# Linear attention inside a three-stage kernel: the sums over keys computed with the features stationary and v, widened by a column of ones, moving

## The chip, the cores and the metric

One core of a Trainium2 chip runs the whole program. The metric is the device time in microseconds of one execution. The kernel before takes 2109.36 us, the median of three runs (2109.34 to 2110.07).

## The reference

Three stages follow each other: attention with exponential features, a squared-ReLU feed-forward layer, and a mixture of eight experts whose gates are balanced by eight row and column normalisations. The change lies in the first stage.

```python
def _attn_ref(q, k, v, w_phi):            # q, k, v: 4 x 8 x 576 x 64; w_phi: 64 x 128
    def phi(x):
        proj = np.einsum('bhsd,df->bhsf', x, w_phi)
        proj = proj - np.max(np.abs(proj), axis=-1, keepdims=True)
        return np.concatenate([np.exp(proj), np.exp(-proj)], axis=-1)
    q_p, k_p = (phi(q), phi(k))
    kv = np.einsum('bhsf,bhsd->bhfd', k_p, v)
    z = np.sum(k_p, axis=2)
    num = np.einsum('bhsf,bhfd->bhsd', q_p, kv)
    den = np.einsum('bhsf,bhf->bhs', q_p, z)[..., None] + 1e-06
    return (num / den).astype(np.float32)

def _moe_ref(x, w_in, w_out):             # x: 2304 x 512, hidden width 2048
    h = np.maximum(x @ w_in, 0.0)
    return (h * h @ w_out).astype(np.float32)
...
```

## The kernel before

**Units.** The attention stage runs over 16 units (NU), each one batch entry and two heads. For a unit, k and v (576 rows a head) lie as four full tiles of 128 rows and one of 64 rows (MT = 4, R0 = 64). q is handled turned, with the features on the partitions.

**Steps of a unit.** Ten small functions, s_kT to s_fin, each write out one step:

- turn_k turns k (tiles pskT), proj_k multiplies it by w_phi (psk), subtracts the largest absolute value and takes both exponentials: ek, rows on the partitions, two heads h, two signs a, 128 features;
- split_q and turn_q turn q (psqT), proj_q makes psq, and, through a reduction over partitions on GpSimd, eq: one tile for each of two halves of the rows (c) and each head (h), features on the partitions, both signs;
- kv_sum (L336) sums over the rows. For each tile and head, v is the stationary operand (64 columns) and ek the moving one (256 columns): kvp, with head h on the partitions 64h to 64h + 63, so that the two heads use the two halves of the array's columns. The sums z come from a second set of matmuls with 32 columns of ones stationary: zp, four groups of 32 partitions for two heads and even and odd tiles. ScalarE copies both to SBUF as kvs;
- kv_turn (L369) turns the four 128 x 128 pieces of kvs on TensorE (kzp), and VectorE copies out kv, adds the two parts of z (zs) and repeats it 32 times (z): now the features are on the partitions;
- numerators (L398) multiplies for each c: four matmuls psn (kv stationary, 64 columns, the two heads in two column tiles, the two signs added up) and four matmuls psd (z stationary, 32 columns, four column tiles); ScalarE copies out nm and dn, and the denominators go through DRAM as comp;
- recip divides, writes rden to DRAM and reads it back on all partitions as rb; finish multiplies nm by rb and writes xh and xl, the two halves of the next stage's input.

**What sets the order.** The steps of all units are sorted by planned times (a unit every TU = 17.54 us, offsets OFFS), and written in that order. A scheduler in the framework then orders every engine's instructions by a simulation of the timeline, so that the instructions of one step may stand apart. PSUM has three banks for the tiles of kv_sum, kv_turn and numerators (pool pc, PCB = 3) and three for those of the turns and projections (pa). v has two buffers (VAB = 2); kv_sum issues the load of v two units ahead, on SyncE's queue, in front of the copies. Into the attention stage the kernel weaves the first pass of the feed-forward layer (first_l1, first_l2; tiles ps, lines 244 to 246): half a batch entry of it can start when the four units of this entry are finished. HOLD keeps some of these halves behind the kv_sum of a named unit, by kv_sum's last instruction.

All operands of kvp, zp, psn and psd are f32. In the trace one such matmul is two instructions, each a weight load (LDWEIGHTS) and a MATMUL; these are called passes here.

## Time and profile before

| | |
|---|---|
| median of three runs | 2109.36 us |
| the profiled execution | 2109.05 us |
| its span | 2107.3 us |
| TensorE busy (PE) | 2065.6 us, 98% |
| weight loads (PEld) | 1929.1 us, 92% |
| VectorE (DVE) | 1734.0 us, 82% |
| ScalarE (ACT) | 873.1 us, 41% |
| GpSimd (POOL) | 767.5 us, 36% |
| TensorE's clock, mean granted share | 0.994 |

The attention stage fills the first 290 us, its end reaches to about 310 us; the rest of the first feed-forward pass goes on to about 350 us, the other passes to 665 us, and the experts fill what is left. Matmuls are pipelined and their ends are modelled, so the distance from one start to the next says more than a busy share. In the rows, PE is the matmul side of TensorE, PEld its weight loads. A matmul's shape such as 128*64 128x256 gives rows and columns of the stationary operand, then partitions and columns of the moving one. "Idle before" in square brackets is the time for which the engine stood still, with what ended it.

### The profile page before, as it was taken

Reading aid. Unit: us, or ns where it says so; the run is one execution under the profiler, and the core shown is the slowest. Engines: PE = TensorE matmul, PEld = TensorE weight load, DVE = VectorE, ACT = ScalarE, POOL = GpSimd, SP = SyncE. Lnnn points to the kernel's source line nnn. Section 1 sums busy time; section 2 is a strip of 40 time slices with the busy share of each in tenths; the row PEclk is TensorE's granted clock in tenths of the full one; section 3 lists DMA queues with packets and bytes.
Section 4 is the critical chain, followed back from the end, with each engine's and each line's share of the span. In section 5 each row is a group of like instructions: output and inputs, shape, how many; then the busy total and the mean of one; then the engine's idle time right before and its main releaser. Section 6 shows DMA issues by size and latency. Waiting matters only on the chain.

```text
span 2107.3 us, 31771 instructions
## 1 busy us (share of the span) xinstructions
PE 2065.6 (98%) x12411; PEld 1929.1 (92%) x12411; DVE 1734.0 (82%) x2154; ACT 873.1 (41%) x1503; POOL 767.5 (36%) x425
## 2 busy tenths in 40 slices
PE   8999999999999999999999999999999999999998
PEld 5556679888999999999999999999999999999998
DVE  4888655766566886998989989899898998989986
ACT  6786744222233654433433333333343333433332
POOL 3343300010104443443544444444444444444431
PEclk9999999999999999999999999999999999999999
DMA  4444231100135456667676776666766666676663
GB/s 112 114 101 120 74 124 60 60 31 31 55 156 206 174 200 216 202 226 253 222 229 206 226 255 220 225 222 222 247 227 220 227 223 238 224 228 234 212 201 122
DMA packets 184052, 376.40 MB, mean 179 GB/s; under 512 B 73440, under 2 KB 114272, under 8 KB 183904
## 3 DMA queue, kind: packets, MB, share of 16 engines
q1 hardware_dynamic: 183904, 374.38, 54.1%
q8 instruction: 99, 1.62, 0.3%
q14 instruction: 49, 0.40, 0.1%
HBM read 349.26 MB, written 24.93 MB: 178 GB/s over the span
## 4 chain that ended last, share of the span: by engine, by line
PE 85%; DVE 8%; DMA 3%; ACT 1%; issue 1%; SPq 1%; POOL 1%; DVEq 0%; ACTq 0%; POOLq 0%
PE psa L858 30%; PE psb L858 30%; PE ps L244 6%; PE ps L245 6%; PE ps L246 6%; PE kvp L353 2%; PE psn L409 1%; PE zp L360 1%; DMA rb<-rden 1%; DVE xl L594 1%; DVE hv L594 1%; PE psd L418 1%; DVE w2v L594 1%; DVE acc L974 1%; DMA xl<-xv 1%
## 5 line engine op out<-in xcount | busy, mean ns | idle before, releaser
L858 PE MATMUL psb<-xl,xh 128*128 128x384 f32 x2400 | 447.7, 336 | 7.4 <-DMA xl<-xv 2.8
L858 PE MATMUL psa<-xl,xh 128*128 128x384 f32 x2400 | 446.1, 335 | 3.3 <-DVE xl L594 2.5
L858 PEld LDWEIGHTS psb<-xl,xh 128*128 128x128 f32 x2400 | 420.4, 189 | 9.3 <-issue 4.2
L858 PEld LDWEIGHTS psa<-xl,xh 128*128 128x128 f32 x2400 | 419.0, 188 | 4.4 <-DVE xl L594 2.9
L886 POOL TENSOR_TENSOR t<-r,r 128x768 f32<-128x768 f32 x96 | 207.4, 2161 | 501.2 <-DVE r L926 452.6
L886 POOL TENSOR_TENSOR t<-r,t 128x768 f32<-128x768 f32 x96 | 233.6, 2434 | 8.8 <-ACT r L930 3.3
L974 DVE TENSOR_TENSOR acc<-psb,acc 128x768 f32<-128x768 f32 x163 | 155.0, 951 | 41.8 <-PE psb L858 38.5
L594 DVE TENSOR_TENSOR xl<-t,xl 128x768 fp32r<-128x768 f32 x128 | 183.1, 1430 | 0.3 <-ACT xl L593 0.2
L974 DVE TENSOR_TENSOR acc<-psa,acc 128x768 f32<-128x768 f32 x161 | 153.1, 951 | 36.4 <-PE psa L858 33.2
L858 PE MATMUL psb<-xl,w2v 128*128 128x384 f32 x960 | 180.4, 334 | 0.0
L858 PE MATMUL psa<-xl,w2v 128*128 128x384 f32 x960 | 180.1, 334 | 0.0
L593 ACT CAST xl<-t 128x768 fp32r<-128x768 f32 x128 | 107.3, 838 | 153.5 <-POOL t L886 62.6
L858 PEld LDWEIGHTS psb<-xl,w2v 128*128 128x128 f32 x960 | 167.6, 188 | 0.0
L858 PEld LDWEIGHTS psa<-xl,w2v 128*128 128x128 f32 x960 | 167.5, 188 | 0.0
L593 ACT CAST xl<-r 128x768 fp32r<-128x768 f32 x96 | 80.4, 838 | 157.1 <-PE psa L858 77.8
L393 POOL PARTITION_ALL_REDUCE eq<-eq x64 | 90.0, 1447 | 138.4 <-ACT eq L392 138.4
L594 DVE TENSOR_TENSOR xl<-r,xl 128x768 fp32r<-128x768 f32 x96 | 137.2, 1430 | 2.3 <-ACT xl L593 2.2
L244 PE MATMUL ps<-xh,w0h 128*128 128x288 f32 (+3 forms) x384 | 131.5, 343 | 3.5 <-ACT r L265 3.5
L245 PE MATMUL ps<-xl,w0h 128*128 128x288 f32 (+3 forms) x384 | 129.6, 338 | 0.0
L246 PE MATMUL ps<-xh,w0l 128*128 128x288 f32 (+3 forms) x384 | 129.4, 338 | 0.0
L245 PE MATMUL ps<-gl,w1h 128*128 128x288 f32 (+3 forms) x384 | 127.3, 338 | 0.0
L246 PE MATMUL ps<-gh,w1l 128*128 128x288 f32 (+3 forms) x384 | 126.7, 338 | 0.0
(195 smaller groups left out, 3742.6 us busy)
## 6 DMA issues: line engine op xcount, KB each, us to landing
xl<-xv SPq DMA_DIRECT2D x329, 768.0 KB
wf<-in_moe_w_dram SPq DMA_DIRECT2D x32, 1024.0 KB
gate<-prT SPq DMA_DIRECT2D x45, 384.0 KB
xv<-xvs SPq DMA_DIRECT2D x14, 768.0 KB
raw<-in_moe_w_in_dram SPq DMA_DIRECT2D x16, 512.0 KB
raw<-in_moe_w_out_dram SPq DMA_DIRECT2D x16, 512.0 KB
xv<-xl SPq DMA_DIRECT2D x7, 768.0 KB
qnat<-in_q_dram SPq DMA_DIRECT2D x16, 288.0 KB
```

The source lines that it names most:

```text
L244: nc.tensor.matmul(ps, ah, bh, start=first, stop=False)
L245: nc.tensor.matmul(ps, ah, bl, start=False, stop=False)
L246: latest["pe"] = nc.tensor.matmul(ps, al, bh, start=False, stop=last).ins
L353: nc.tensor.matmul(kvp[h * D : (h + 1) * D, : 2 * NF], t[:r, i, h], e, start=(i == 0), stop=(i == MT))
L360: ins = nc.tensor.matmul(zp[q0 : q0 + 32, : 2 * NF], ones[:r, :32], e, start=(i < 2), stop=(i >= MT - 1))
L393: nc.gpsimd.partition_all_reduce(eq[:, 1], eq[:, 0], P, bass_isa.ReduceOp.absmax)
L409: nc.tensor.matmul(ps[h * D : (h + 1) * D, :HALF], kv[:, a, h * D : (h + 1) * D], eqs[2 * c + h][:, a], start=(a == 0), stop=(a == 1),)
L593: nc.scalar.copy(v[:, 0], src)
L594: nc.vector.tensor_sub(v[:, 1], src, v[:, 0].bitcast(F32))
L858: ins = nc.tensor.matmul(ps[:, x, :NB], w[:, wi, k, cs], b[:, bi, k], start=first and k + i == 0, stop=k == KH - 1 and i == 2, skip_group_ ...
L886: nc.gpsimd.tensor_tensor(t[nm], x, y, ALU.subtract)
L974: latest["dve"] = nc.vector.tensor_add(o, ps, o).ins
```

## The change

kv_sum keeps its loops over tiles and heads but swaps the operands: ek is stationary (128 features, for each sign), and v moves, 64 columns and a 65th of ones. The four results (two signs, two heads), each 128 partitions by 65 columns, lie side by side in one PSUM bank, kvz, and are summed over the tiles there; one start flag opens the bank. kv_out, in the place of kv_turn, copies kv and the repeated z straight out of it on VectorE. The copies kvs, the turns kzp and the sum zs are gone. v's tile gets 65 columns instead of 64, and load_kv writes ones into the last with a memset on GpSimd ahead of the load. numerators reads kv by its new shape.

```diff
@@ -120,22 +120,24 @@
         nc.sync.dma_start(t, heads(q, u).rearrange("h s d -> (h s) d").rearrange("(t p) d -> p t d", p=P))
         nat["q", u] = t
 
-    def load_kv(u, src, nm, bufs):
+    def load_kv(u, src, nm, bufs, w):
 
         if u >= NU:
             return
-        t = ab.tile([P, MT + 1, 2, D], F32, tag=f"n{nm}", bufs=bufs, name=f"{nm}nat")
+        t = ab.tile([P, MT + 1, 2, w], F32, tag=f"n{nm}", bufs=bufs, name=f"{nm}nat")
+        if w > D:
+            nc.gpsimd.memset(t[:, :, :, D:], 1.0)
         src = heads(src, u)
         for h in range(2):
-            nc.sync.dma_start(t[:, :MT, h], src[h, : MT * P].rearrange("(p t) d -> p t d", t=MT))
-        nc.sync.dma_start(t[:R0, MT], src[:, MT * P :].rearrange("h p d -> p h d"))
+            nc.sync.dma_start(t[:, :MT, h, :D], src[h, : MT * P].rearrange("(p t) d -> p t d", t=MT))
+        nc.sync.dma_start(t[:R0, MT, :, :D], src[:, MT * P :].rearrange("h p d -> p h d"))
         nat[nm, u] = t
 
     def load_k(u):
-        load_kv(u, k, "k", 2)
+        load_kv(u, k, "k", 2, D)
 
     def load_v(u):
-        load_kv(u, v, "v", VAB)
+        load_kv(u, v, "v", VAB, D + 1)
 
     load_k(0)
 
@@ -336,49 +338,26 @@
 
     def kv_sum(u, eks):
 
-
         t = nat.pop(("v", u))
-        kvp = pc.tile([P, 512], F32, tag="pc", name="kvp")
-        zp = pc.tile([P, 512], F32, tag="pc", name="zp")
-
-        def rows(i, h):
+        ps = pc.tile([P, 512], F32, tag="pc", name="kvz")
+        ps = ps[:, : 4 * (D + 1)].rearrange("p (a h d) -> p a h d", a=2, h=2)
+        for i in range(MT + 1):
             r = P if i < MT else R0
-            return r, eks[i // GT][:r, i % GT, h].rearrange("p a f -> p (a f)")
-
-        for g in range(0, MT + 1, 2):
-            tiles = range(g, min(g + 2, MT + 1))
-            for i in tiles:
-                for h in range(2):
-                    r, e = rows(i, h)
-                    nc.tensor.matmul(
-                        kvp[h * D : (h + 1) * D, : 2 * NF], t[:r, i, h], e, start=(i == 0), stop=(i == MT)
-                    )
-            for i in tiles:
-                for h in range(2):
-                    r, e = rows(i, h)
-                    q0 = 32 * (2 * (i % 2) + h)
+            for h in range(2):
+                for a in range(2):
+
                     ins = nc.tensor.matmul(
-                        zp[q0 : q0 + 32, : 2 * NF], ones[:r, :32], e, start=(i < 2), stop=(i >= MT - 1)
+                        ps[:, a, h], eks[i // GT][:r, i % GT, h, a], t[:r, i, h],
+                        start=(i == h == a == 0), stop=(i == MT), skip_group_check=True,
                     )
         load_v(u + VAB)
-        kvs = ab.tile([P, 2, 2, NF], F32, tag="kvs", name="kvs")
-        nc.scalar.copy(kvs[:, 0].rearrange("p a f -> p (a f)"), kvp[:, : 2 * NF])
-        nc.scalar.copy(kvs[:, 1].rearrange("p a f -> p (a f)"), zp[:, : 2 * NF])
-        return kvs, ins.ins
-
-    def kv_turn(u, kvs):
-        ps = pc.tile([P, 2, 2, P], F32, tag="pc", name="kzp")
-        for i in range(2):
-            for a in range(2):
-                nc.tensor.transpose(ps[:, i, a], kvs[:, i, a], ident)
-        kv = ab.tile([P, 2, P], F32, tag="kv", bufs=2, name="kv")
-        zs = ab.tile([P, 2, 2], F32, tag="zs", bufs=1, name="zs")
+        return ps, ins.ins
+
+    def kv_out(u, ps):
+        kv = ab.tile([P, 2, 2, D], F32, tag="kv", bufs=2, name="kv")
         z = ab.tile([P, 2, 2, 32], F32, tag="z", bufs=2, name="z")
-        nc.vector.tensor_copy(kv, ps[:, 0])
-        nc.vector.tensor_reduce(
-            zs, ps[:, 1].rearrange("p a (g h r) -> p a h g r", g=2, h=2)[:, :, :, :, 0], AX.X, ALU.add
-        )
-        nc.vector.tensor_copy(z, zs.rearrange("p a (h o) -> p a h o", o=1).to_broadcast([P, 2, 2, 32]))
+        nc.vector.tensor_copy(kv, ps[:, :, :, :D])
+        nc.vector.tensor_copy(z, ps[:, :, :, D:].to_broadcast([P, 2, 2, 32]))
         return kv, z
 
     def proj_q(qT):
@@ -407,7 +386,7 @@
             for a in range(2):
                 for h in range(2):
                     nc.tensor.matmul(
-                        ps[h * D : (h + 1) * D, :HALF], kv[:, a, h * D : (h + 1) * D], eqs[2 * c + h][:, a],
+                        ps[h * D : (h + 1) * D, :HALF], kv[:, a, h], eqs[2 * c + h][:, a],
                         start=(a == 0), stop=(a == 1),
                     )
             nc.scalar.copy(nm[:, c], ps[:, :HALF])
@@ -480,7 +459,7 @@
         U[u]["kvs"], U[u]["kvi"] = kv_sum(u, U[u].pop("ek"))
 
     def s_kz(u):
-        U[u]["kz"] = kv_turn(u, U[u].pop("kvs"))
+        U[u]["kz"] = kv_out(u, U[u].pop("kvs"))
 
     def s_num(u):
         U[u]["nm"], U[u]["comp"] = numerators(u, U[u].pop("kz"), U[u].pop("eq"))
```

The engines' orders, before and after. First TensorE from the numerators of unit 3 to the sums of unit 4; psk, psq, pskT and psqT are the projections and turns of neighbouring units. Before, the sums of unit 4:

```order
L311 MATMUL pskT<-ident,knat 128x128 x4
L353 MATMUL kvp<-ek,vnat 64x256 x10
L311 MATMUL pskT<-ident,knat 128x64
L298 MATMUL psqT<-ident_r,qst 128x128 x4
L360 MATMUL zp<-ek,ones 32x256 x10
L298 MATMUL psqT<-ident_r,qst 128x128 x4
L373 MATMUL kzp<-ident,kvs 128x128 x2
L298 MATMUL psqT<-ident_r,qst 128x128
```

After, the same place:

```order
L349 MATMUL kvz<-vnat,ek 128x65 x8
L368 MATMUL psq<-qT,wks 128x288
L369 MATMUL psq<-qT,wks 128x288
L313 MATMUL pskT<-ident,knat 128x128 x4
L313 MATMUL pskT<-ident,knat 128x64
L349 MATMUL kvz<-vnat,ek 128x65 x12
L300 MATMUL psqT<-ident_r,qst 128x128 x9
```

The sums are now in two runs, the second in one piece behind the turns of k, and the turns kzp that stood among the turns of q are gone.

The second place is the numerators of unit 3, also on TensorE. Before, the first half and the start of the second, which goes on in the same way:

```order
L409 MATMUL psn<-eq,kv 64x288 x4
L389 MATMUL psq<-qT,wks 128x288
L390 MATMUL psq<-qT,wks 128x288
L418 MATMUL psd<-eq,z 32x288 x4
L409 MATMUL psn<-eq,kv 64x288 x4
```

After, from the second instruction group of the first half on (a single psn and a single psd of this half stand ahead of it, with four groups of psk in between):

```order
L388 MATMUL psn<-eq,kv 64x288 x3
L397 MATMUL psd<-eq,z 32x288 x3
L246 MATMUL psk<-wdh,kh 64x256
L247 MATMUL psk<-wdl,kh 64x256
L248 MATMUL psk<-wdh,kl 64x256
L388 MATMUL psn<-eq,kv 64x288
L397 MATMUL psd<-eq,z 32x288
L388 MATMUL psn<-eq,kv 64x288 x3
L397 MATMUL psd<-eq,z 32x288 x3
```

Each half's four psn and four psd stood together; now one of each stands ahead and three behind, in both halves of this unit. Counted over the whole program, an unbroken run of psn occurs 37 times before and 55 times after, of psd 35 and 55 times (32 of each would leave every half whole); stretches of column-tiled matmuls (kvp, zp, psn, psd) between others number 88 and 60. Ahead of the last psd stand 337 matmuls of the feed-forward layer in either order.

On GpSimd one memset of vnat (128 x 10) stands for each unit between the four reductions eq and the next cast qst; it waits for the last sum of the unit that used the buffer.

## Rows read from the trace of the kernel before

**Rows 1.** Busy time by stretch: us, each engine (instructions), PE clock, DMA, GB/s

```profile
50.00:100.00 50.00, 47.03 (x395) 28.62 (x387) 43.19 (x92) 39.94 (x103) 19.77 (x17) 1.00 0.48 116
100.00:150.00 50.00, 48.13 (x397) 29.56 (x397) 45.09 (x96) 39.97 (x105) 21.16 (x15) 1.00 0.41 104
150.00:200.00 50.00, 45.80 (x369) 29.60 (x365) 40.52 (x80) 34.16 (x90) 19.86 (x14) 0.97 0.45 112
200.00:250.00 50.00, 50.00 (x382) 34.00 (x382) 35.30 (x78) 34.37 (x88) 13.52 (x11) 1.00 0.33 87
300.00:350.00 50.00, 46.49 (x330) 46.05 (x329) 18.32 (x41) 19.26 (x46) 0.00 (x0) 0.93 0.37 115
```

**Rows 2.** Timeline at 153 us: start, us, engine, instruction, [idle before]

```profile
153.57 0.76 DVE L439 TENSOR_TENSOR nm<-nm,rb 128x576 f32<-128x576 f32 x1 [3.07 <-DMA rb<-rden]
...
155.38 1.12 PE L353 MATMUL kvp<-ek,vnat 128*64 128x256 f32 x4 [2.56 <-ACT dn L421]
```

**Rows 3.** Chain that ended last, sums of two units: start, us, what

```profile
16.01 1.01 PE kvp L353 x8
17.03 0.57 PE zp L360 x8
17.60 0.58 PE kvp L353 x4
18.18 0.55 PE zp L360 x4
...
46.22 2.46 PE kvp L353 x20
...
49.35 1.55 PE zp L360 x20
```

**Rows 4.** The chain again: turns, and numerators of the first unit

```profile
19.95 0.22 PE kzp L373 x2
...
26.15 0.65 PE psd L418 x6
```

**Rows 5.** Timeline of the gate's logits (psg), loads, then matmuls

```profile
573.45 1.48 PEld L635 LDWEIGHTS psg<-wg,acc 128*128 128x128 f32 x12
574.85 0.19 PEld L244 LDWEIGHTS ps<-xh,w0h 128*128 128x128 f32 x1
...
573.62 1.40 PE L635 MATMUL psg<-wg,acc 128*128 128x8 f32 x12
574.87 0.43 PE L244 MATMUL ps<-xh,w0h 128*128 128x384 f32 x1
```

**Rows 6.** Timeline of PE, numerators of the first unit, second half

```profile
27.62 0.70 PE L409 MATMUL psn<-eq,kv 128*64 128x288 f32 x2
28.25 0.67 PE L418 MATMUL psd<-eq,z 128*32 128x288 f32 x2
28.85 0.40 PE L389 MATMUL psq<-qT,wks 128*128 128x288 f32 x1
29.09 0.30 PE L390 MATMUL psq<-qT,wks 128*128 128x288 f32 x1
...
29.36 0.29 PE L390 MATMUL psq<-qT,wks 128*128 128x288 f32 x1
29.59 1.08 PE L353 MATMUL kvp<-ek,vnat 128*64 128x256 f32 x8
```

**Rows 7.** The chain, numerators of the last unit

```profile
284.07 1.12 PE psn L409 x8
285.19 0.62 PE psd L418 x8
...
288.25 1.11 PE psn L409 x6
289.36 0.67 PE psd L418 x8
```

**Rows 8.** Groups by shape on POOL, first 312 us: count, busy, mean ns, idle before

```profile
L393 POOL PARTITION_ALL_REDUCE eq<-eq x64 | 90.0, 1447 | 138.4 <-ACT eq L392 138.4
```

## The prediction

> **What bounds the kernel now.** I read the busy time by stretch first, then TensorE's own timeline inside the attention stage, then the chain of waits. The change touches only the attention stage, the first 310 us; behind it the program is the same work in nearly the same order. So the question is what the attention stage is short of. From 50 to 200 us PE is idle 2.97, 1.87 and 4.20 us of each 50, about 9.0 in all; from 200 us on the same view has it at 50.00 of 50. ACT is near 40 of 50 and DVE at most 45 [rows 1]. PE is therefore the limit for most of the stage, and a microsecond of PE work added there is nearly a microsecond of time, apart from what the 9 us of gaps can swallow. What the gaps are is seen at 153 us: DVE's nm waits 3.07 us for the DMA that brings back the reciprocals, ACT's queue stands behind it, and PE, which needs the PSUM bank that ACT's copy dn frees, waits 2.56 us [rows 2]. Such waits run on other clocks than PE's. The stage's end is one more: 3.51 us idle and a granted clock of 0.93 in 300 to 350 us, a mean of its levels 2.4 and 1.2 GHz [rows 1], while the last unit's reciprocals go through DRAM.
>
> I price PE work by the distance from one matmul's start to the next one's start, since ends are modelled and busy times overlap.
>
> **Part 1: the sums themselves.** Before, a unit has ten kvp matmuls, ten zp, and four turns. In one piece each, kvp takes 2.46 and zp 1.55 us, 4.01 together; cut in five pieces, 1.01 + 0.57 twice and 0.58 + 0.55, 4.29 [rows 3]. Two turns take 0.22, so four take about 0.45 [rows 4]. That is 4.5 to 4.7 a unit; I take 4.6, times 16 units 73.6 us (bounds 71.4 to 76).
>
> After, a unit has twenty f32 matmuls with 128 stationary and 65 moving columns. The trace of before has no such row, but it has the gate's logits: f32, 128 stationary columns, only 8 moving. One f32 matmul is two passes there, each with its own load: 12 passes stand 0.117 us apart by the loads and 0.104 by the matmuls [rows 5]. With 8 moving columns it is the load that sets this, so a pass costs at least that. That 65 moving columns hide behind the load I take from the turns, where 128 moving f32 columns went through at 0.11 us a piece [rows 4]: 65 should need about half. I take 0.112 us, 40 passes a unit, 640 in all: 71.7 us (bounds 66.6 to 74.9). The last tile has only 64 rows, a change of array mode into it and out; by the price of other mode changes below, 0.2 us a unit, 3.2 us (bounds 0 to 3.2). So the sums cost 74.9 after against 73.6: **+1.3 us** (bounds -9 to +7). Column tiles are why the old form is not dearer for all its columns: with 256 of them moving, kvp's passes come at 1.01 / 8 = 0.126 us each and zp's at 0.57 / 8 = 0.07 [rows 3].
>
> The Trainium skill, page "TensorEngine Tiling", section "Performance Considerations", advises for 64 or fewer columns of the right operand to swap the two operands and tile by columns. The kernel before does just that with v's 64 columns, and the change undoes it; the rule speaks against the change, and rows 3 and 5 agree that nothing is won by it. The page "TensorE: Matmul & The Clock Gate" of the Trainium skill, section "LDWEIGHTS (loading the stationary operand)", makes a load cost its columns at 1.2 GHz, 107 ns for 128; by it the 640 passes would be 68.3 us and the sum above -2.1 instead of +1.3.
>
> **Part 2: how the numerators are cut.** This is the largest term, and it comes from the order, not from the new function. kv and z are there earlier, without the copies kvs and the turns. The scheduler then issues the first numerator matmul (psn, h = 0) and its denominator (psd) as soon as the first eq is ready, and the other three later. Before, PE's order has psn in 37 runs and psd in 35 (32 would be whole); after, 55 and 55. Such cuts stand in the first and the last unit of before: a lone psn (two passes) takes 0.63 us, a lone psd 0.60, the three others 1.11 and 0.65, where a whole psn takes 1.12 and a whole psd 0.62 [rows 4, 6, 7]. A cut thus costs 0.62 for psn and 0.60 to 0.63 for psd: the lone half has no partner in the other column tile. 18 x 0.62 + 20 x 0.60 = **+23.2 us** (bounds 23 to 25).
>
> **Part 3: mode changes.** The first matmul behind column-tiled ones stands 0.24 us from its follower, the last one ahead of them 0.23, and those in between 0.135 [rows 6]: 0.20 a run. PE's order has 88 column-tiled runs before and 60 after, since the sums no longer belong to them: 28 x 0.20 = **-5.6 us** (bounds -6 to -5).
>
> **Part 4: the other engines.** ACT loses the two copies kvs of every unit, DVE a small reduction. Neither bounds the stage [rows 1], so this is worth nothing directly; the shorter path from sums to kv helps where PE has nothing else to do, in the first unit, by about its turns and copies: **-1.5 us** (bounds -2 to 0). POOL gets a memset of ten columns per unit. It waits for the previous use of the v buffer, that is for PE's last kvz of the same unit; behind it in POOL's queue stands the next CAST qst, which waits for PE's later turns anyway, and on SP the load of v two units ahead. Even at the price of POOL's reductions (1.45 us), 16 of them are 23 us against 138 us in which POOL waits for ACT [rows 8]. Nothing.
>
> **Part 5: waits.** PE comes later by some 17 us over 290, the DMA round trip and the decoding on DVE do not. So part of the 9.0 us of gaps fills up, and with it 1.5 us that the granted clock of 0.97 in 150 to 200 us costs [rows 1]. The wait at 153 us [rows 2] is of that kind; others, for banks and for eq, come back with the new order. I take **-7 us** (bounds -10.5 to +3; below nothing saved, since every cut adds a place where PE can wait). The end of the stage stays: 337 matmuls of the feed-forward stand ahead of the last psd in both orders, so the same work covers the last round trip.
>
> Sum: 1.3 + 23.2 - 5.6 - 1.5 - 7 = +10.4 us. The profiled execution took 2109.05 us (span 2107.3), the median is 2109.36: the forecast is 2119.5 us, slower by 0.5%. Its own range is 2113 to 2130.
>
> **Rivals.**
> (a) *Hidden.* The lone matmuls stand where PE would have waited, so the gaps swallow most: all 10.5 us, and the sums come out at their lower price, 0.104 a pass (-5 us). Then 23.2 - 5.6 - 2 - 10.5 - 4 = about +1: 2110, no change. For it: the scheduler cuts where it believes PE idle. Against: from 200 us on there is no gap [rows 1], and a third of the new cuts lie there.
> (b) *Faster, by moving columns.* If the load of the next pass hides, and the 65 columns set the pace, a pass costs half of a turn's 0.11, 0.055 us: 640 x 0.055 + 3.2 = 38.4, so the sums fall by 35 and the whole by 19 before waits, about 12 when the other engines become the limit: 2090 to 2097. It decides from a pass below 0.089 us, where the sum of the parts reaches -4.2. Against: 8 moving columns took 0.104 to 0.117 [rows 5]. The Trainium skill, page "TensorE: Matmul & The Clock Gate", section "Back-to-back issue gap", prices a matmul that way in its table by free dimension; it adds itself that this counts too little where loads are not hidden.
> (c) *Faster, by waits.* One bank instead of three and no copies in between could remove bank waits like the one at 153 us, and more of the clock's fall: 2100 to 2105. Against: kvz still takes the bank that dn frees.
> (d) *Much slower.* Load and matmul of a pass do not overlap: 0.055 more on 640 passes, +35: about 2154.
>
> **Chances.** Forecast 0.62, (a) 0.18, (b) 0.08, (c) 0.06, (d) 0.06. A measurement of this kernel can tell 0.2%, 4.2 us. Slower by more: 0.62 + 0.06 = 0.68; within: 0.18; faster: 0.14. The range from 2106 to 2131 holds the forecast and (a).
>
> **What would show it.** kvz passes 0.10 to 0.12 us apart in the timeline (step 1; 0.055 is (b), 0.165 is (d)); lone psn and psd of two passes at 0.6 us each, in twenty places more than before (step 2); the last psd of unit 15, at 289.4 us before [rows 7], some 8 to 13 us later; PE's gaps in 50 to 200 us below 9 us. The forecast is wrong if the last psd comes no later, or if the stretch behind 320 us changes its length.

## The result, and the profile after

The changed kernel takes 2137.17 us (median of 4 executions, 2132.8 to 2138.08) where the kernel before took 2109.72 us beside it: a ratio of 1.0125, with an interval of 1.011 to 1.014. It is slower by 27.5 us. The forecast had 10.4 us, and the time lies above the top of its range, 2131. The profiled execution took 2136.38 us (span 2134.6).

The chain of waits of the changed kernel, in order of time, at the end of the attention stage (columns: start us, us, what):

```profile
302.40 2.77 PE kvz L349 x24
...
308.56 0.63 PE psn L388 x2
309.19 0.60 PE psd L397 x2
309.80 1.11 PE psn L388 x6
310.91 0.62 PE psd L397 x6
313.05 0.63 PE psn L388 x2
314.13 0.60 PE psd L397 x2
316.52 1.11 PE psn L388 x6
317.64 0.65 PE psd L397 x6
```

The last unit's psd starts at 317.64 us, at 289.36 before [rows 7]: 28.3 us later. What lies behind it is as long as before within 1 us, since the span grew by 27.3 us. So the loss is in the attention stage alone. There one sees the cuts that the prediction spoke of: a lone psn 0.63, a lone psd 0.60, in both numerator groups of the unit.

Busy time by stretch of the changed kernel (columns as in [rows 1], which it answers to):

```profile
0.00:50.00 50.00, 43.64 (x246) 31.42 (x249) 22.33 (x50) 27.83 (x66) 13.32 (x22) 0.86 0.43 106
50.00:100.00 50.00, 49.41 (x342) 33.83 (x337) 34.76 (x73) 35.48 (x90) 20.11 (x19) 0.97 0.41 99
100.00:150.00 50.00, 48.55 (x324) 38.92 (x324) 39.32 (x79) 31.27 (x81) 16.83 (x16) 0.86 0.35 90
150.00:200.00 50.00, 47.76 (x339) 34.92 (x335) 40.14 (x80) 34.50 (x86) 19.64 (x17) 0.93 0.34 85
200.00:250.00 50.00, 50.00 (x369) 38.50 (x369) 39.29 (x79) 32.88 (x83) 13.29 (x14) 1.00 0.49 127
250.00:300.00 50.00, 50.00 (x353) 38.47 (x352) 30.73 (x63) 29.36 (x75) 12.41 (x11) 1.00 0.22 60
300.00:350.00 50.00, 47.91 (x333) 41.51 (x333) 28.20 (x61) 20.90 (x52) 4.08 (x4) 1.00 0.42 131
```

From 50 to 200 us PE idles 4.3 us instead of 9.0: the gaps were filled, as forecast. But the last column but two, the granted clock, is new. It was 1.00, 1.00 and 0.97 there before; now it is 0.97, 0.86 and 0.93. A busy PE gets through half as many passes at 1.2 GHz, as the rows below show, and the busy column does not show it. In this execution the records of the clock have 37.5 us at 1.2 GHz up to the last psd (before, 3.4 us; the 10.2 us of the expectations below count a stretch behind the last psd too). One such stretch, on PE's timeline (start us, us, engine, line, operation, tiles and shape, xcount):

```profile
118.78 2.11 PE L349 MATMUL kvz<-vnat,ek 128*128 128x65 f32 x14
120.65 0.59 PE L368 MATMUL psq<-qT,wks 128*128 128x288 f32 x1
121.04 0.44 PE L369 MATMUL psq<-qT,wks 128*128 128x288 f32 x1
121.28 1.35 PE L313 MATMUL pskT<-ident,knat 128*128 128x128 f32 x5
122.56 3.67 PE L349 MATMUL kvz<-vnat,ek 128*128 128x65 f32 x16
125.99 0.59 PE L246 MATMUL ps<-xh,w0h 128*128 128x288 f32 x1
```

Sixteen passes of kvz stand 3.43 us long here (from 122.56 to the next start at 125.99), 0.214 each; at 2.4 GHz sixteen took 1.70 in other places of this trace. No row has an idle time in it: PE had work all the while.

**How the rest of this text counts.** I take the profiled execution of a kernel from its start to its last psd and split this time in three.

- *Idle* is the time in which PE stood still.
- *Clock* is half of the time in which PE was busy at 1.2 GHz. The time ahead of the first record of the clock (10.0 to 29.9 us) counts as 1.2 GHz, since passes take twice their time there too: eight kvp passes of the kernel before took 1.97 us at 12.02 us and 1.01 later [rows 3].
- *Work* is what is left: what the passes take at 2.4 GHz, with cuts, changes of mode, and waits too short to show as idle.

PE's busy time in these stretches, before and after (columns as in [rows 1]):

```profile
0.00:289.60 289.60, 273.91 (x2144) 174.20 (x2144) 216.15 (x458) 207.02 (x533) 102.18 (x85) 0.99 0.39 100
0.00:317.80 317.80, 307.17 (x2077) 229.43 (x2080) 218.87 (x446) 200.28 (x501) 99.68 (x101) 0.94 0.36 92
```

The kernel before has 267.7 us of work, 6.2 of clock and 15.7 of idle, 4.6 of it the wait for the first load. The table has the differences to it in us. Work, clock and idle add up to the shift of the last psd. *Time* is the median against the kernel before in executions beside it. *Mean clock* is (1 - mean granted clock of all of a kernel's executions) x 2110 us, 12.5 us before (mean 0.9941 over some 80 executions); it reaches over the whole execution and leaves out the time ahead of the first record.

| kernel | time | last psd | work | clock | idle | mean clock | runs of psn / psd |
|---|---|---|---|---|---|---|---|
| changed kernel | +27.5 | +28.3 | +18.2 | +15.1 | -5.0 | +5.4 | 55 / 55 |
| e1: head 1 first | +11.0 | +14.3 | -6.4 | +13.9 | +6.9 | +7.0 | 34 / 37 |
| e2: 128 columns | +28.4 | +30.4 | +30.9 | +1.6 | -2.1 | +0.2 | 63 / 61 |
| e3: both | +1.5 | +2.9 | -7.0 | +3.0 | +6.9 | +1.0 | 32 / 35 |
| e4: before, cut by hand | +24.3 | +25.0 | +31.0 | -3.6 | -2.3 | -4.1 | 64 / 65 |
| e5: e1 with 8 columns | +43.7 | +45.9 | -16.1 | +53.9 | +8.2 | +53.4 | 33 / 39 |
| e6: e3, fewer kvz | -8.1 | -2.8 | -30.2 | +12.6 | +14.8 | +11.0 | 34 / 35 |
| e7: e3, fifth eq buffer | +1.3 | +0.5 | -9.3 | +3.2 | +6.6 | +1.8 | 33 / 32 |
| e8: e3, copies on ACT | +5.2 | +5.5 | -7.3 | +4.1 | +8.7 | +4.6 | 32 / 33 |
| e9: e3, 32 ones | +7.1 | +8.3 | -7.0 | +5.1 | +10.2 | +5.1 | 33 / 34 |
| e10: e9, kvz first | +7.4 | +8.3 | -6.8 | +7.4 | +7.8 | +7.1 | 32 / 35 |
| e11: before, head 1 first | +8.9 | +8.6 | -0.4 | +1.0 | +8.0 | +3.5 | 36 / 32 |
| e12: before, numerators early | +1.5 | +4.3 | -1.1 | +1.4 | +4.1 | +1.0 | 38 / 35 |
| e13: before, fewer ones | -11.9 | -8.8 | -5.8 | -4.0 | +0.9 | -2.0 | 42 / 38 |
| e14: changed, numerators early | +34.0 | +40.8 | +16.2 | +15.4 | +9.2 | +10.7 | 55 / 53 |
| e15: e3, numerators early | +0.3 | +1.9 | -8.2 | +2.0 | +8.1 | +0.8 | 32 / 32 |
| e16: e9, numerators early | +7.9 | +8.7 | -8.2 | +7.2 | +9.7 | +5.9 | 33 / 33 |

The split is that of one execution of each kernel, and good to 2 or 3 us; in e5 the work comes out some 10 us below e1's for nearly the same passes, so there the clock is put too high by as much.

### The profile page after: what moved, and what is told of

It is laid out like the page before. It is cut to its first block, busy times and chain, and to the rows that moved or that the text cites. A ratio compares the mean times of both kernels' runs of the same rounds, so it can differ in the third digit from the quotient of the medians.

```text
span 2134.6 us, 31646 instructions
## 1 busy us (share of the span) xinstructions
PE 2099.5 (98%) x12347; PEld 1984.4 (93%) x12347; DVE 1733.7 (81%) x2138; ACT 866.2 (41%) x1471; POOL 763.6 (36%) x441
## 3 DMA queue, kind: packets, MB, share of 16 engines
q1 hardware_dynamic: 183904, 374.38, 53.9%
## 4 chain that ended last, share of the span: by engine, by line
PE 89%; DVE 6%; DMA 2%; ACT 1%; issue 1%; SPq 0%; POOL 0%; DVEq 0%; ACTq 0%
PE psa L837 30%; PE psb L837 30%; PE ps L246 6%; PE ps L247 6%; PE ps L248 6%; PE kvz L349 3%; PE psn L388 2%; PE psd L397 1%; DVE xl L573 1%; DVE hv L573 1%; PE psqT L300 1%; DMA xl<-xv 1%; DVE acc L953 1%; PE psk L246 1%; PE psg L614 1%
```

## The experiments

### Where the loss sits: cuts, columns or gaps (e1 to e5)

e1 turns the loop over the heads round in the numerators; e2 lets 128 columns move in a pass of kvz; e3 does both.

```diff
-                for h in range(2):
+                for h in (1, 0):
```

```diff
-                        ps[:, a, h], eks[i // GT][:r, i % GT, h, a], t[:r, i, h],
+                        ps[:, a, h], eks[i // GT][:r, i % GT, h, a],
+                        t[:r, i].rearrange("p h d -> p (h d)")[:, 2 * h : 2 * h + P],
```

> The changed kernel with the loop over the two heads of psn and psd turned round (head 1 first), which lets the scheduler cut them less: psn in 34 runs of passes (changed kernel 55), psd in 37 (55). The arithmetic is the changed kernel's. Three theories of where the changed kernel lost 13.7 us that my sum had not: TensorE at 1.2 GHz for 37.5 us of the attention stage, where the kernel before had 10.2 us. COLUMNS: the level falls in and behind stretches of kvz passes, because a pass of kvz is mostly a weight load (0.107 to 0.112 us) with 65 columns moving behind it. Then 39 cuts fewer at 0.61 us take 24 us off and the level still falls: 2137 - 24 = 2113 (2107 to 2119), 25 us or more at 1.2 GHz in the stage. CUTS: it falls because a lone pass of psn or psd uses a half or a quarter of the columns of the array. Then both go: 2137 - 24 - 14 = 2099 (2094 to 2105), at most 14 us at 1.2 GHz. GAPS: it falls where TensorE waited shortly before. Then each stretch at 1.2 GHz has an idle of over 1 us in the 10 us ahead of it, whatever it runs.

Measured: 2120.43 us, ratio to the kernel before 1.0051 (1.0034 to 1.0068). 39 cuts fewer took 24.6 us of work off, 24 were expected, and 16.7 us of time. The clock did not come back. The records have 17.1 us at 1.2 GHz up to the last psd, less than the 25 that COLUMNS asked for and more than the 14 that CUTS allowed. But here the first record comes at 29.9 us only, and the passes ahead of it take twice their time:

```profile
16.69 4.55 PE L349 MATMUL kvz<-vnat,ek 128*128 128x65 f32 x20
21.18 0.61 PE L368 MATMUL psq<-qT,wks 128*128 128x288 f32 x1
```

Twenty kvz passes stand 4.5 us long. With this time it is 47.0 us, against 48.3 in the changed kernel counted likewise. On PE's timeline of e1, an idle (in brackets, with what ended it) ahead of the first stretch in the records, and two blocks of kvz in it:

```profile
81.98 0.37 PE L368 MATMUL psq<-qT,wks 128*128 128x288 f32 x1 [1.28 <-DVE ek L333]
...
84.18 3.40 PE L349 MATMUL kvz<-vnat,ek 128*128 128x65 f32 x16 [0.51 <-ACT ek L335]
...
89.25 5.57 PE L349 MATMUL kvz<-vnat,ek 128*128 128x65 f32 x24
```

The 1.2 GHz level holds through both blocks with the cuts gone. But GAPS asked for an idle of over 1 us in the 10 us ahead of each stretch, and e1's two stretches have one, 1.28 and 1.64 us. So e1 alone does not decide between COLUMNS and GAPS. The time, 2120, lies a microsecond above the range of COLUMNS. PE idles 11.9 us more than in the changed kernel, and its largest new wait is psn's for the features, which the changed kernel does not have (engine, line, releaser: us in total, times, longest us):

```profile
PE psn L388 <- ACT eq L375: 4.8, 6, 2.5
```

> The changed kernel with 128 columns moving behind each weight load of kvz instead of 65 (the v tile of both heads beside each other; the sums of the other head are computed too and left unread), and four copies out of PSUM for each unit instead of two. psn falls in 63 runs here and psd in 61 (changed kernel 55 and 55). A pass stays at its load, 0.11 us. COLUMNS: the level no longer falls by kvz, at most 10 us at 1.2 GHz in the attention stage: 2137 - 14 to 19 + 14 cuts at 0.61 (8.5) = 2129 (2123 to 2135). CUTS: more cuts, so at least 37 us at 1.2 GHz: 2137 + 8.5 = 2146 (2140 to 2152). GAPS: the level falls only behind an idle of TensorE of over 1 us.

Measured: 2137.81 us, 1.013 (1.0114 to 1.0146), no faster than the changed kernel. The records have 6.8 us at 1.2 GHz in the stage, as COLUMNS said, and the clock column is back at the level of the kernel before. The time did not follow, and lies above the 2135 that COLUMNS allowed: this order has 12.7 us more work than the changed kernel, which takes back the 13.5 us of the clock. 14 more cuts account for 8.5 of it by their price, and twenty-four passes with the 64-row tile stand 2.96 to 3.07 us here instead of 2.86 to 2.96, some 2 us in all; the others are not accounted for.

> Both edits together: 128 columns behind each load of kvz, and head 1 first in psn and psd (psn in 32 runs, psd in 35). COLUMNS: at most 10 us at 1.2 GHz, and 43 cuts fewer than the changed kernel at 0.61: 2137 - 26 - 14 to 19 = 2095 (2090 to 2101), faster than the kernel before (2109.7). CUTS gives much the same time, 2097, and shows itself by the two kernels with one edit each. If neither is the cause, 25 us or more stay at 1.2 GHz and the time is 2137 - 26 = 2111 (2107 to 2117).

Measured: 2110.97 us, 1.0008 (0.9999 to 1.0018), the time of the kernel before, 9.5 us below e1, of whose cuts it has all but four. COLUMNS had 2090 to 2101 and at most 10 us at 1.2 GHz, and the records have 13.7: as a forecast of the time it failed. The comparison with e1 still speaks for it: work and idle are the same within 0.6 us, and the last psd comes 11.4 us earlier, 10.9 of them clock (6.0 by the means). It is no win over the kernel before, although it has 7 us less work: PE idles 6.9 us more.

e4 cuts the numerators of the kernel before by hand, its sums untouched: the first pass of psn, then that of psd, then the others, with both PSUM banks of a group taken ahead of the first pass.

```diff
+            for part in (order[:1], order[1:]):
+                for a, h in part:
+                  with tc.issue_after(last) if last is not None else ExitStack():
```

> The kernel before (kvp and zp as they were, no kvz) with psn and psd cut by hand: of each group the first pass of psn, then the first of psd, then the rest of psn, then the rest of psd. psn falls in 64 runs (before 37), psd in 65 (35). The arithmetic is the kernel before's. 57 cuts at 0.61 are 34.8 us: 2109.7 + 34.8 = 2144 (2136 to 2150) if a cut costs only itself, as COLUMNS says, with at most 14 us at 1.2 GHz in the attention stage (before 10.2). CUTS: the level falls too, 30 us or more at 1.2 GHz: 2144 + 10 or more = 2154 (2150 to 2165).

Measured: 2133.73 us, 1.0109 (1.0094 to 1.0124). 57 more cuts add 31.0 us of work and 24.3 us of time, 0.54 and 0.43 us each; 2136 to 2150 was expected. Busy time by stretch of e4 (the clock is the third number from the end):

```profile
50.00:100.00 50.00, 48.81 (x362) 26.98 (x365) 38.28 (x82) 36.90 (x94) 19.14 (x15) 1.00 0.42 97
100.00:150.00 50.00, 48.92 (x352) 28.76 (x346) 39.76 (x85) 34.85 (x89) 15.00 (x12) 1.00 0.39 98
150.00:200.00 50.00, 48.16 (x359) 30.15 (x356) 40.92 (x85) 36.07 (x94) 16.96 (x14) 1.00 0.42 111
```

With more cuts than the changed kernel the clock does not fall once in the stage: CUTS, as a cause by itself, is out. On GAPS e4 says nothing, since PE has no idle over 1 us in it behind the start. The changed kernel does. Rows with the idles ahead of two of its stretches, which begin at 58.5 and 120.0 us:

```profile
57.89 0.39 PE L246 MATMUL psk<-wdh,kh 128*128 128x256 f32 x1 [0.24 <-ACT qT L301]
...
118.51 0.66 PE L349 MATMUL kvz<-vnat,ek 128*128 128x65 f32 x4 [0.52 <-ACT ek L335]
```

In the 10 us ahead of its stretches at 58.5, 120.0 and 181.4 us PE's longest idle was 0.24, 0.52 and 0.56 us, not over 1, so there GAPS does not hold. (The stretch at 14.1 us lies too near the start to tell: an idle of 0.99 us and the end of the wait for the first load stand ahead of it.) As a second cause GAPS is not out. In the kernel before and in e12 each of the three stretches up to the last psd stands behind an idle of 2.3 to 2.6 us, and in e3, e7 and e15 eight of nine stand behind one of 1.3 to 1.7.

e5 is e1 with 8 columns moving instead of 65:

```diff
-                        ps[:, a, h], eks[i // GT][:r, i % GT, h, a], t[:r, i, h],
+                        ps[:, a, h, D - 7 :], eks[i // GT][:r, i % GT, h, a], t[:r, i, h, D - 7 :],
```

> e1_whole with only 8 columns moving behind each weight load of kvz (7 features of v and the ones) instead of 65; the other 57 features are left out of the sums. psn falls in 33 runs and psd in 39 (e1: 34 and 37), so the cuts stay. Up to its last psd e1 stood at 1.2 GHz for 47 us (29.9 us ahead of the first record of the clock, where its passes take twice their time, and 17.1 us in the records); e3 with 128 columns for 25.7 us. COLUMNS: a pass stays at its load, 0.105 to 0.112 us, and with less moving the level falls more: 60 us or more at 1.2 GHz, 2120 + 6 to 20 = 2126 to 2140, slower for moving fewer columns. LOADS (a rival: the level falls by weight loads, whatever moves behind them, and e3 had less of it by its other order): 40 to 54 us, 2114 to 2124. If a pass follows its columns, it is shorter than 0.09 us and the time goes below 2112.

Measured: 2154.49 us, 1.0199 (1.0181 to 1.0217): 34 us slower than e1 for moving fewer columns, and 14 us beyond what COLUMNS expected. One block on PE's timeline of e5, at 2.4 GHz:

```profile
192.87 1.85 PE L349 MATMUL kvz<-vnat,ek 128*128 128x8 f32 x16
194.57 0.38 PE L368 MATMUL psq<-qT,wks 128*128 128x288 f32 x1
```

From 192.87 to 194.57 are 1.70 us for sixteen passes, 0.106 each. Sixteen with 65 columns took 1.70, and so did sixteen with 128 in e3:

```profile
109.57 1.95 PE L349 MATMUL kvz<-vnat,ek 128*128 128x128 f32 x16
111.27 0.38 PE L246 MATMUL ps<-xh,w0h 128*128 128x288 f32 x1
```

So 8, 65 and 128 moving columns cost the same: the load sets the pass. Busy time by stretch of e5:

```profile
0.00:50.00 50.00, 41.26 (x249) 31.58 (x249) 21.99 (x47) 27.68 (x67) 12.55 (x21) 0.80 0.46 112
50.00:100.00 50.00, 43.63 (x272) 33.08 (x273) 28.37 (x63) 29.17 (x73) 16.50 (x16) 0.72 0.29 76
100.00:150.00 50.00, 48.69 (x313) 38.20 (x315) 40.83 (x81) 31.78 (x80) 13.24 (x14) 0.76 0.38 97
150.00:200.00 50.00, 44.37 (x299) 33.24 (x296) 33.13 (x68) 28.72 (x71) 17.22 (x16) 0.78 0.30 73
200.00:250.00 50.00, 49.45 (x345) 39.15 (x345) 38.32 (x79) 32.94 (x83) 13.96 (x15) 0.88 0.44 119
250.00:300.00 50.00, 50.00 (x375) 41.75 (x374) 29.99 (x64) 30.88 (x79) 12.69 (x14) 0.93 0.27 72
```

The clock is below 1.00 in every stretch: 126 us at 1.2 GHz in the records up to the last psd, 137 with the time ahead of the first one, against 47.0 in e1. Twelve of the 17 stretches have no idle over 0.3 us in the 10 us ahead. Loads are those of e1 and cuts nearly so, so LOADS is out and the moving columns count. (That e5 also feeds other values into the numerators, since 57 features are missing, was not tested apart.) In executions as a whole the clock lost 65.9 us in e5 and 19.5 in e1, 46 us apart, and the time differs by 34.

That 65 columns are few enough shows in the first 30 us. The kernels with 65 or 8 moving columns (changed kernel, e1, e5, e14) stand at 1.2 GHz for 24.4 to 29.9 of them, all others, with 128 columns or the old sums, for 10.0 to 16.7, but for e17, which waits for GpSimd. Later in the stage the order counts too. Over whole executions e2, e3, e7 and e15, with 128 columns, lost 13 to 14 us to the clock, but e8, e9 and e16 17 to 18 and e10 20; with 65, the changed kernel lost 17.9, e1 19.5, e14 23.2.

### Why less work than before is no faster (e6 to e10)

e6 is e3 with kvz over row tiles 0, 2 and 4 alone; e7 is e3 with `EQB = 5` and one buffer for z; e8 has the copies of kv and z on ScalarE.

```diff
-        for i in range(MT + 1):
+        for i in (0, 2, 4):
```

```diff
-    EQB = 4
+    EQB = 5
...
-        z = ab.tile([P, 2, 2, 32], F32, tag="z", bufs=2, name="z")
+        z = ab.tile([P, 2, 2, 32], F32, tag="z", bufs=1, name="z")
```

```diff
-            nc.vector.tensor_copy(kv[:, :, h], ps[:, :, h, o : o + D])
+            nc.scalar.copy(kv[:, :, h], ps[:, :, h, o : o + D])
```

> e3_wide_whole with kvz over three of the five row tiles alone (the sums over k leave the other two out): 256 passes less at 0.112 us, 28.7 us of TensorE's work. The question is why e3, with some 15 us less work of TensorE in the attention stage than the kernel before, takes the time of the kernel before. FEED: the waits for the features of q and k set the pace in the first 200 us and fill up what is taken away: at most 12 us faster than e3, 2099 to 2108, and TensorE's waits in the stage rise by more than 15 us. TENSORE: its work and its clock set the end, and e3's loss lies in the clock: 25 to 32 us faster, 2079 to 2086.

> e3_wide_whole with five buffers for the features of q (eq) instead of four, and one for z instead of two to make room. psn in 33 runs, psd in 32 (e3: 32 and 35). The four tiles of a unit fill the four buffers, so psq of the next unit waits until psn and psd have read this unit's, and psn waits for the last of its features. FEED: a fifth buffer takes 5 to 12 us of waits off: 2099 to 2106, faster than the kernel before. TENSORE: no change from e3, 2108 to 2113.

> e3_wide_whole with the copies of kv and z out of PSUM on ScalarE instead of VectorE: 4 copies of 279 and 212 ns for each unit, 982 ns, leave VectorE (42 of 50 us busy between 50 and 200 us) and come to ScalarE (36 of 50). psn in 32 runs, psd in 33. FEED BY VECTORE: VectorE sets the pace of the first 200 us (TensorE's longest waits there are for the subtraction of ek), so some 11 units of 0.98 us come off: 2111 - 5 to 11 = 2100 to 2106. If it is no single engine but the chain of a unit from one engine to the next, moving work between two of them changes little: 2107 to 2114.

Measured: e6 2102.69 us, 0.9958 (0.9946 to 0.9971); e7 2112.11, 1.001 (0.9995 to 1.0024); e8 2115.2, 1.0016 (1.0005 to 1.0026). e6 gave up 23 us of work against e3 and gained 8 us, in the range of FEED; but PE idles 8 us more, not the 15 that FEED asked for. Where the rest went is in its stretches:

```profile
50.00:100.00 50.00, 44.35 (x315) 30.12 (x315) 42.88 (x94) 37.54 (x96) 22.19 (x19) 0.93 0.43 109
100.00:150.00 50.00, 44.87 (x326) 32.79 (x325) 41.61 (x92) 37.63 (x95) 18.96 (x18) 0.93 0.41 105
150.00:200.00 50.00, 42.46 (x286) 32.35 (x285) 39.23 (x81) 32.30 (x82) 17.03 (x16) 0.86 0.40 102
```

PE idles 18 us of these 150, 11 in e3, and the clock is lower too. So of 23 us of work some 10 came back as lost clock and 8 as idle. No single feeder was found: a fifth buffer for the features of q changed nothing (e7), and VectorE relieved of its copies made it no faster (e8 is 4 us above e3 and above both of its ranges, with 3.6 us more lost to the clock by its mean).

e9 puts 32 columns of ones between the heads of v; e10 besides writes kvz ahead of the q projection.

```diff
-        t = ab.tile([P, MT + 1, 2, w], F32, tag=f"n{nm}", bufs=bufs, name=f"{nm}nat")
+            t = ab.tile([P, MT + 1, D + 32 + D], F32, tag=f"n{nm}", bufs=bufs, name=f"{nm}nat")
+            nc.gpsimd.memset(t[:, :, D : D + 32], 1.0)
...
-                        t[:r, i].rearrange("p h d -> p (h d)")[:, 2 * h : 2 * h + P],
+                        t[:r, i, 32 * h : 32 * h + P],
```

```diff
-    (9.28, 'kv')
+    (6.5, 'kv')
```

> e3_wide_whole with 32 columns of ones between the two heads of v, so that the sums of ones come out already repeated 32 times: still 128 columns behind each load, and two copies of 192 columns for each unit instead of four (by the rows some 2 x 340 ns instead of 982 ns). Four DMA loads of v for a unit instead of three. psn in 33 runs, psd in 34. The clock stays where e3 had it (25 us at 1.2 GHz up to the last psd, 15 to 35). FEED BY VECTORE: 0.3 us less for each unit, 2 to 5 us faster than e3: 2106 to 2109. The chain of a unit: 2108 to 2113.

> e9 with the passes of kvz of a unit written ahead of its q projection instead of behind it (kvz in 31 runs of passes instead of 38). psq waits for a PSUM buffer until VectorE has read psk; with kvz between psk and psq that wait has something to cover it. If that wait is what the first 200 us lose: 3 to 8 us faster than e9, 2101 to 2107. If kvz then waits for the last exponentials of k instead, and stands in one block that the clock falls in: no faster, 2109 to 2118, with more than 30 us at 1.2 GHz.

Measured: e9 2117.06 us, 1.0029 (1.0019 to 1.0039); e10 2117.41, 1.003 (1.0019 to 1.0041). e9 is a miss: fewer copies on VectorE did not help, and it is 6 us above e3, with 4 us more lost to the clock by its mean. e10 came out as its second case says, no faster and with 36.4 us at 1.2 GHz up to its last psd, the time ahead of the first record counted in. But e9 had 30.7 counted so, and in the records alone both have 20.5, so the block of kvz is not shown to be the reason.

### What the order alone is worth, and what fewer ones are worth (e11 to e16)

e11 is the kernel before with `for h in (1, 0)` in the numerators; e12, e14, e15 and e16 have the numerators written earlier (e12 from the kernel before, e14 from the changed one, e15 from e3, e16 from e9):

```diff
-    (23.24, 'num')
+    (20.7, 'num')
```

> The kernel before with head 1 first in psn and psd, and nothing else: the same instructions with the same work, in another order on the engines (psn in 36 runs and psd in 32, before 37 and 35). A control: what a change of the order alone is worth in a kernel whose offsets were set for another order. ORDER: the kernel before stands on an order that suits it, and any other loses some us in its first 200 us: 2113 to 2119. WORK: the order is worth nothing and 4 cuts fewer give 2 us: 2106 to 2110.

> The kernel before with the step of the numerators of a unit written ahead of the next unit's k projection (offset 20.7 instead of 23.24), with psn in 38 runs and psd in 35 (37 and 35): a second control with the same instructions in another order. ORDER: 2113 to 2119. WORK: 2108 to 2112.

Measured: e11 2118.82 us, 1.0046 (1.0032 to 1.006), slower by 8.9 us with the same instructions and the same work within half a microsecond. e12 2111.33, 1.0004 (0.9995 to 1.0014), no difference. What PE waited for in the first 300 us of e11 (columns: engine, line, releaser: us in total, times, longest us):

```profile
PE psq L389 <- DVE ek L331: 3.5, 5, 1.3
PE psn L409 <- DVE kv L377: 1.6, 2, 1.1
PE pskT L311 <- ACT eq L392: 1.4, 2, 0.9
PE psqT L298 <- DVE kl L314: 1.3, 2, 0.7
PE psn L409 <- ACT eq L396: 1.2, 2, 0.8
PE psd L418 <- ACT dn L421: 1.1, 1, 1.1
```

In the kernel before, psq waited for DVE's ek 0.8 us in all where it is 3.5 here, and for pskT on ACT's eq and psd on ACT's dn it had no such row; its longest, kvp on ACT's dn, fell from 4.5 us to 0.9. In all PE idles 8.0 us more, spread over many short waits. In e1 psn's wait for the features of q (eq) was the largest new one, 4.8 us; here it is 1.2, so why this order waits more is not shown. The same cost stands in e1: against the changed kernel 25 us of work came off, and PE's idle took 12 us back. ORDER holds for e11 and not for e12: an order can cost 9 us, and need not.

e13 runs zp over the first two row tiles alone, in the kernel before:

```diff
-            for i in tiles:
+            for i in tiles if g == 0 else ():
```

> The kernel before with the separate sums of ones over the first two of the five row tiles alone (the other rows are left out of the denominators): 96 of 160 matmuls of zp less, some 16 us of TensorE's work (zp in 1.553 us for a run of ten matmuls). psn in 42 runs and psd in 38, 8 more than before, +5 us. This is the gain that the change was after, without its new kind of pass. FEED: the features of q and k set the pace of the first 200 us, so little of it shows: 2106 to 2112. TENSORE: 2110 - 16 + 5 = 2099 (2096 to 2103).

Measured: 2098.95 us, 0.995 (0.9933 to 0.9966), 11.9 us faster; 11 were expected if TensorE's work sets the time. zp fell from some 27 to 10.2 us, and psn, psd and kvp rose by some 7 with their cuts. In the trace the work is 5.8 us less and the clock lost 4.0 less, so that the time came out as expected is in part luck. But PE idles no more than before (+0.9): what is taken off the work shows in full. So in the kernel before TensorE's work is the bound, as the prediction read it from [rows 1], and FEED as a rule for the stage is out. At most it describes the orders that begin with head 1.

> The changed kernel with the step of the numerators written earlier (offset 20.7 instead of 23.24), the edit of e12; same instructions, psn in 55 runs and psd in 53 (55 and 55). ORDER: the changed kernel's own order is a bad one, and another gives another time, 5 us or more from 2137 to either side: below 2132 or above 2142. CUTS AND CLOCK: with the same cuts and the same passes 2133 to 2140.

> e3_wide_whole with the same edit; psn in 32 runs, psd in 32 (32 and 35). ORDER: 5 us or more from e3's 2111: it may fall to 2100 to 2106 and beat the kernel before, or stand above 2116. CUTS AND CLOCK: 3 cuts fewer, 2107 to 2112.

> e9_wide32 with the same edit; psn in 33 runs, psd in 33 (33 and 34). ORDER: 5 us or more from e9's 2117: 2106 to 2112, or above 2122. CUTS AND CLOCK: 2114 to 2119.

Measured: e14 2144.8 us, 1.0159 (1.0136 to 1.0181); e15 2111.15, 1.0005 (0.9995 to 1.0015); e16 2118.68, 1.0034 (1.0019 to 1.0049). Of these three, only the changed kernel moved with the edit, as ORDER says for it; e15 and e16 lie where CUTS AND CLOCK has them. Against the kernel before beside it e14 lost 6.5 us more than the changed kernel with its own order. By the mean 5 us more of TensorE's time went to the clock; the profiled execution, the slowest of four, has 14 us more idle instead.

### Fewer sums of ones without the new passes (e17, e18)

In the kernel before, two row tiles of features are added ahead of zp, on GpSimd (e17) or VectorE (e18), so that zp runs over three tiles:

```diff
+            if len(tiles) == 2:
+                e2 = eks[g // GT]
+                nc.gpsimd.tensor_add(e2[:, 0], e2[:, 0], e2[:, 1])
```

> The kernel before with the features of two row tiles of k added on GpSimd (in place, behind their kvp passes) ahead of the sums of ones, so that zp runs over three tiles instead of five: 64 of 160 matmuls less at 0.155 us (1.553 us for a run of ten), 9.9 us of TensorE's work; psn in 34 runs and psd in 34 (37 and 35), 2.4 us. 32 additions of 512 columns on GpSimd, which is busy 20 of 50 us. TENSORE: 2110 - 12 = 2098 (2095 to 2103), faster than both kernels. If the additions stand in the way of the maxima over the partitions, or hold the buffers of the features of k too long: 2106 to 2118.

> The same with the additions on VectorE, which is busy 43 of 50 us between 50 and 150 us: 32 more operations of 512 columns at 0.59 us or so, 19 us for VectorE in the stage. psn in 37 runs, psd in 36, so 9.9 us of TensorE's work less. TENSORE: 2100 (2097 to 2104). If VectorE's load sets the pace of the first 200 us: 2110 to 2122.

Measured: e17 2385.22 us, 1.1291 (1.1276 to 1.1307), far above both of its ranges; e18 2121.43, 1.0046 (1.0033 to 1.0059). Both expectations priced zp wrongly. With two row tiles its four matmuls stand abreast in four column tiles, and eight passes take 0.57 us, but four take 0.55 [rows 3]. One tile at a time leaves two of the four empty: in e18 zp fell from some 27 us to 25.5, not by 9.9. The additions on VectorE (0.82 us each) then only cost: psq waited 7.5 us for DVE's ek, 0.8 before, and the time lies in the second range of e18.

e17's loss is GpSimd's. Its timeline (in brackets the idle ahead of a row, and what ended it):

```profile
103.62 1.25 POOL L358 TENSOR_TENSOR ek<-ek 128x512 f32<-128x512 f32 x1 [7.63 <-issue]
110.65 1.25 POOL L393 PARTITION_ALL_REDUCE eq<-eq  x1 [5.79 <-issue]
118.75 1.25 POOL L358 TENSOR_TENSOR ek<-ek 128x512 f32<-128x512 f32 x1 [6.85 <-issue]
119.97 0.65 POOL L287 CAST qst<-qnat 128x576 fp32r<-128x576 f32 x1
```

The maximum over the partitions is PARTITION_ALL_REDUCE. At each change shown between it and the addition the second stands 5.8 to 7.6 us behind the first with nothing to wait for; a CAST behind an addition follows at once. PE waited 207.3 us for these additions. The Trainium skill, page "GPSIMD Engine Reference", section "2.1 Instruction dispatch", puts about 6 us on the first call to a freshly loaded kernel. The trace agrees in the size, with 5.79 and more, but has it at each change; that it is the same cost is not shown.

No kernel here beat the kernel before with the whole of its arithmetic.

## Why the prediction was wrong

**Part 1** held. Forty passes of a unit take 1.70 us for sixteen and 2.86 for the twenty-four with the 64-row tile and its changes of mode, 4.56 together, 73.0 us for 16 units; the forecast had 74.9. The old sums come to 73 or 74 counted likewise, the forecast had 73.6. Rivals (b) and (d), 0.055 or 0.165 us a pass, are out by e5 and e3: the load sets 0.106, whatever moves.

**Part 2** held: by the lengths of their runs at 2.4 GHz psn rose from 38.7 to 49.7 us and psd from 21.7 to 33.6, 22.9 together, against 23.2. e4 shows the same kind of price on the old sums, 31.0 us for 57 cuts.

**Part 3** can't be measured by itself; its price of 0.20 a run stands in the changed kernel's trace as well (a pass of psq ahead of psn is 0.225 us from its follower, ahead of kvz 0.132). **Part 4**'s -1.5 us can't be told apart. Parts 1 to 3 together had +18.9 us of work, and the trace has +18.2.

**Part 5 is the step that failed**, in what it had for the clock. It took -7 us, out of 9.0 of gaps and 1.5 of lost clock that goes with them (bounds -10.5 to +3). In the profiled execution the gaps did fill: PE idles 5.0 us less up to the last psd, and 4.3 us in 50 to 200 us where "below 9" was said. But the clock cost 15.1 us more where a saving of up to 1.5 stood: +10.1 together, beyond the upper bound. Up to its last psd TensorE stood at 1.2 GHz for 48.3 us, 18.7 before, the time ahead of the first record counted in both. 18.2 + 15.1 - 5.0 is the 28.3 us by which the last psd came later. What I left out is that the new passes, a load each with few columns behind it, draw TensorE's clock down (e3 against e1, e5, and the first 30 us of all kernels), and that PE loses time there without any idle to show. I had priced the old loss of clock as something to be filled up, and did not ask what the new work would do to it, though [rows 5] showed passes of that kind.

This split is that of one execution of four. Over all, 27.5 - 18.2 leaves +9.3 us for clock and waits together, where parts 4 and 5 had -8.5, and the two partly stand in for each other. The four executions had mean clocks of 0.987, 0.991, 0.992 and 0.996, a spread of 19 us of TensorE's time, and took 2136.4, 2138.0, 2138.1 and 2132.8. Part of this spread can lie ahead of the first record, which no mean holds: e1's came 19 us later than the changed kernel's. Over the executions of the kernel before, a microsecond lost to the clock goes with some 0.6 us of time. So even the best-clocked execution is 23 us behind.

Two things stay open: what the other three executions of the changed kernel lost to waits and what to the clock, since they have no trace, and how much of its clock belongs to its order. By their means e14 lost another 5 us to the clock by an order alone.

Rival (a) is out: the gaps that it counted on did fill, and the loss is seen all the same; e4 shows 24 of 31 us of cuts in the time. Rival (c) is out with part 5, of which it was the hopeful end.

## What to carry to other kernels

An f32 pass with 128 stationary columns costs its load, 0.106 us, from 8 to 128 moving columns (e5, the changed kernel, e3); a form that exchanges long moving rows for many loads wins nothing in passes and can lose in the clock. Before forecasting that new work fills gaps, look what the granted clock does in the stretches of the old trace that hold work of the new kind. And a change that makes an operand ready earlier may let the scheduler cut column-tiled groups: count the runs, which here cost 0.5 to 0.6 us of work and 0.43 of time each.

## What the runs showed of the hardware

- TensorE's clock fell with no idle of PE over 0.56 us in the 10 us ahead (three stretches of the changed kernel), and with 8 moving columns, twelve times with none over 0.3. The Trainium skill, page "TensorE: Matmul & The Clock Gate", section "HAM oscillation — how this bites in real kernels", tells of falls by waits for data. The kernel before agrees, with a wait of 2.56 us ahead of its fall; the changed kernel and e5 do not, and here the measurement decides.
- With the same loads, 8 moving columns had 126 us at 1.2 GHz in the records and lost 46 us more than 65.
- The load of a pass takes twice its time at 1.2 GHz too: 0.214 us for kvz against 0.106.
- Ahead of the first record of the clock (10 to 30 us into the span) passes also take twice their time: 1.97 us for eight kvp passes of the kernel before against 1.01.
- On GpSimd, a change between an addition and a maximum over the partitions costs 5.8 to 7.6 us (e17).
